# A gated feed-forward kernel whose gated values are stored with three of nine blocks as sums of three, and a last stage in another order

## The chip, the cores and the metric

One core of one Trainium2 chip. The metric is the device time of one execution in microseconds (us); lower is better.

## What is computed

Causal attention with a window of 128 and a linear position bias over 8 batches, 8 heads, 576 positions and 64 dimensions a head; its output, 4608 tokens of 512 features, goes through a gated feed-forward layer of 1536 hidden units. All of it is float32.

```python
gate = 1.0 / (1.0 + np.exp(-(x @ w_gate)))
val = x @ w_val
return (gate * val @ w_out).astype(np.float32)
```

## The kernel before, in words

The order of all work is written by a planner at build time: `Graph` (L97) takes every operation with an engine, an estimated cost, its reads, writes, a rank and a release time, plays them through against engines that each do one thing at a time, and emits the instructions in the order of their planned start. On the chip each engine's queue runs in that order and waits where it must. All plain transfers are issued on SyncE's queue (`move`, L225), the accumulating ones, which add to what lies at their destination, on GpSimd's (L936).

The work has three stages. In the first (to about 294 us) attention is computed in transposed form, and the first four of twelve hidden blocks of 128 (`ffn`, L657) are projected for the first 3072 tokens. GpSimd makes the attention's masks there (L601). In the second (`ffn2`, L797) the rest of the projections runs in five groups of two halves of tokens (three groups of 2 x 512, two of 2 x 384). It works with fast 2 x 2 block products (7 instead of 8, L850), one chunk for each hidden block and group. A chunk takes 42 matmuls. For each half the gate is a tanh on ScalarE (`gate`, L860), the gated value `(tanh + 1) * val` is made on VectorE (`gated`, L864), and `put` (L644) stores it to DRAM, to a scratch array called `hid`. The gated halves lie in buffers `later_hs`: two in turn, four in the last group. The first thing that a later chunk writes there is a copy by ScalarE of a product out of PSUM (L872, with `copy` of L221).

The third stage is `last` (L921), called for three passes `t` of 1536 tokens. It computes the product with `w_out`: six blocks of `w_out` (2 halves of the outputs m by 3 thirds of the hidden units k) against nine blocks of gated values (3 thirds k by 3 blocks of 512 tokens n). This goes by a scheme of 15 block products instead of 18. Each product takes a sum of blocks of `w_out` (made beforehand by `prepare_o`, L736, stored, and fetched by `fetch_o`, L781), and a sum of blocks of gated values, and is accumulated into one of six running sums ("chains" A to F) in PSUM; outputs are combined from these.

A product (L988) consists of 24 matmuls of 128x512 in float32r: two output blocks j, two quarters q, two rows of 128, three high/low combinations. For each quarter ScalarE makes the high part of the input (L996) and VectorE subtracts it for the low part (L997, through the helper `minus`, L230), in a ring of four buffers `duo`, thus two products. `load` (L925) brings a block of gated values (two transfers of 512 KB) to a free slot; eleven slots exist. `more` (L934) adds a second block to it by an accumulating transfer. `sums` (L939) adds or subtracts whole rows on VectorE (two instructions, L942). After a product, `snap` (L962) copies a running sum out on ScalarE, and `plus` (L968) and `both` (L974) combine results on VectorE; `store` (L982) writes an output block.

In the kernel before, five of the fifteen inputs are made by a plain load, an accumulating load on top of it and a subtraction:

```python
load("f", 0, 0)
more("f", 2, 1)
sums("f", "20", "f", sub)
product(5, "A", "f", lambda j: (plus("y00", "A", "b1", j), store("y00", 0, 0, j)))
```

Of the kernel before, what the change touches and what calls it, by code (L numbers as in the profile page):

```python
# [8 lines left out]
F32 = mybir.dt.float32  # L9
# [6 lines left out]
P = 128  # L16
# [26 lines left out]
OUT0, OSTEP = 425.0, 48.0  # L43
# [35 lines left out]
ORDER = (11, 6, 13, 7, 12, 8, 5, 14, 10, 2, 1, 0, 3, 9, 4)  # L79
# [5 lines left out]
           ((4, (1, 1), SUB, (0, 1)), (9, (1, 0), ADD, (1, 1))))  # L85
SINGLES = ((10, (1, 0)), (2, (0, 1)), (5, (0, 2)), (14, (1, 2)))
# [113 lines left out]
def attention_gated_ffn(ctx: ExitStack, tc: tile.TileContext, qd, kd, vd, wg, wv, wo, out):  # L200
# [85 lines left out]
    for p in range(1, NPAIR):  # L286
# [5 lines left out]
    hid = {(k, q, t): dram.tile([P, 2, NB], F32, name=f"hid{k}{q}{t}")  # L292
           for k in range(3) for q in range(2) for t in range(NB9)}
# [349 lines left out]

    def put(fc, a, b, src, keys, F):  # L644
# [12 lines left out]
    def ffn(t, w):  # L657
# [29 lines left out]
        for i0 in range(0, n, GRP):  # L687
            grp = range(i0, min(n, i0 + GRP))
            for i in grp:
                s = project("g", i)  # L690
                sg = lambda i=i: T(moe, f"sg{i % GRP}", [P, NB], F32)
                g.add("ACT", act_cost(wd, psum=True), lambda s=s, sg=sg: nc.scalar.activation(sg()[:, 0:wd], mm[s][:, 0:wd], AF.Tanh, scale=0.5),
                      [("mm", s)], [("sg", i % GRP)], F)
            for i in grp:
                s = project("v", i)
                sg = lambda i=i: T(moe, f"sg{i % GRP}", [P, NB], F32)
                e = slim[0] % 2
                slim[0] += 1
                h = lambda e=e: hs(e, "early_hs")
                g.add("DVE", dve_cost(wd, psum=True), lambda s=s, sg=sg, h=h: nc.vector.scalar_tensor_tensor(  # L700
                    h()[:, 0:wd], sg()[:, 0:wd], 1.0, mm[s][:, 0:wd], op0=ALU.add, op1=ALU.mult), [("sg", i % GRP), ("mm", s)], [("hs", e, 0), ("hs", e, 1)], F)
                put(w.fcs[i], t * NB, end, lambda a, b, h=h: h()[:, a - t * NB:b - t * NB], [("hs", e, 0), ("hs", e, 1)], F)
# [33 lines left out]
    def prepare_o(kt, want, release):  # L736
# [4 lines left out]
        decode(wo, kt, gt, kg, want, release)  # L741
        for k in (1, 2):
            decode(wo, 4 * k + kt, lambda k=k: tt()[:, 2 * k - 2:2 * k].rearrange("p a f -> p (a f)").bitcast(I32), kt0, want, release + step / 3 * k)
# [3 lines left out]
        for n, batch in enumerate(BATCHES):  # L747
# [7 lines left out]
            for o, (p, a, op, b) in enumerate(batch):  # L755
                va, vb, vo = val(a), val(b), val(p)
                g.add("DVE", dve_cost(2 * P, two=True), lambda va=va, vb=vb, vo=vo, op=op: nc.vector.tensor_tensor(vo(), va(), vb(), op=op),
                      [key(a), key(b)], [("wtmp", z, o)], want, port=True, release=release + (n + 1) * step)
            for o, (p, *_) in enumerate(batch):
                y, i = at_o(p, kt)  # L760
                if y < len(SLOTS):
                    move(lambda y=y, i=i: stash_o[y][:, i], lambda v=val(p): v(), [("wtmp", z, o)], [("stash_o", y, i)], want, 128)
                    continue
                hi, lo, v = (lambda o=o, z=z: six(z)[:, o, 0]), (lambda o=o, z=z: six(z)[:, o, 1]), val(p)
                g.add("ACT", act_cost(2 * P), lambda hi=hi, v=v: nc.scalar.copy(hi(), v()), [("wtmp", z, o)], [("wtmp", z, "hi", o)], want)
                g.add("DVE", dve_cost(2 * P, two=True), lambda hi=hi, lo=lo, v=v: nc.vector.tensor_tensor(lo(), v(), as32(hi()), op=SUB),
                      [("wtmp", z, "hi", o)], [("wtmp", z, o)], want, port=True)
                move(lambda y=y, i=i: stash_o[y][:, i:i + 2], lambda z=z, o=o: as32(six(z))[:, o], [("wtmp", z, o), ("wtmp", z, "hi", o)],
                     [("stash_o", y, i)], want, 256)
        for p, y in SINGLES:  # L770
            z, i = at_o(p, kt)
            move(lambda z=z, i=i: stash_o[z][:, i], block[y], [kt0 if y[1] else kg], [("stash_o", z, i)], want, 128)
# [24 lines left out]
    def ffn2(t, w, todo, F, ends=False):  # L797
# [40 lines left out]
        def chunk(i, fc):  # L838
# [21 lines left out]
            def gate(b, h):  # L860
                g.add("ACT", act_cost(N2, psum=True), lambda: nc.scalar.activation(sg[h](), bk(b)(), AF.Tanh, scale=0.5),  # L861
                      [("mm", b)], [("sg", h)], F)
# [58 lines left out]
    def last(t):  # L921
# [3 lines left out]
        def load(name, k, n):  # L925
            slots = [stage_free.pop(0) for _ in range(2)]
            rows[name] = slots
            for q, slot in enumerate(slots):
                move(lambda slot=slot: staged(slot), lambda q=q: hid[k, q, 3 * t + n], hid_keys(k, n, q), [("row", *slot)], F, 512, True)

        def hid_keys(k, n, q):
            return [y for y in g.writer if y[0] == "hid" and y[1] // 2 == 2 * k + q and y[2] == 3 * t + n]

        def more(name, k, n):  # L934
            for q, slot in enumerate(rows[name]):
                g.add("POOL", 1.2, lambda slot=slot, q=q: nc.gpsimd.dma_start(staged(slot), hid[k, q, 3 * t + n], accum_op=ALU.add),  # L936
                      hid_keys(k, n, q), [("row", *slot)], F, size=512 / 300.0, port=False)
# [30 lines left out]
        def plus(o, chain, a, j, scale=0.5):  # L968
            b, va = bks[chain, j], val((a, j))
            g.add("DVE", dve_cost(NB, psum=True), lambda: nc.vector.scalar_tensor_tensor(va(), mm[b], scale, va(), op0=ALU.mult, op1=ALU.add),  # L970
                  [("mm", b)], [key((a, j))], F)
            held_at[o, j] = held_at.pop((a, j))

        def both(o, a, b, op, j):  # L974
            va, vb = val((a, j)), val((b, j))
            g.add("DVE", dve_cost(NB, two=True), lambda: nc.vector.tensor_tensor(va(), va(), vb(), op=op), [key((b, j))], [key((a, j))], F, port=True)
            held_at[o, j] = held_at.pop((a, j))
# [4 lines left out]
        def store(name, m, n, j):  # L982
            r, c = (2 * m + j) * P, (3 * t + n) * NB
# [4 lines left out]
        def product(p, chain, name, then):  # L988
            ring = []
            for q in range(2):  # L990
# [5 lines left out]
                copy(hi, v, 2 * NB, [("row", *slot)], [("ar", r, 0)], F)  # L996
                minus(lo, v, lambda hi=hi: as32(hi()), 2 * NB, [("row", *slot), ("ar", r, 0)], [("ar", r, 1)], F, pool=False)  # L997
# [19 lines left out]
        add, sub = ALU.add, ALU.subtract  # L1017
        load("10", 1, 0)
        product(11, "A", "10", lambda j: snap("a1", "A", j))
        load("00", 0, 0)  # L1020
        product(6, "B", "00", lambda j: snap("b1", "B", j))
        load("21", 2, 1)
        sums("10", "21", "10", sub)
        product(13, "A", "10", lambda j: snap("a2", "A", j))
        drop("10")
        load("22", 2, 2)
        sums("00", "22", "00", sub)
        product(7, "B", "00", lambda j: snap("b2", "B", j))
        drop("00")
        product(12, "A", "21", lambda j: snap("a3", "A", j))  # L1030
        drop("21")
        product(8, "B", "22", lambda j: snap("b3", "B", j))
        drop("22")
        load("20", 2, 0)
        load("f", 0, 0)
        more("f", 2, 1)
        sums("f", "20", "f", sub)
        product(5, "A", "f", lambda j: (plus("y00", "A", "b1", j), store("y00", 0, 0, j)))
        drop("f")
        load("g", 1, 0)  # L1040
        more("g", 2, 2)
        sums("g", "20", "g", sub)
        drop("20")
        product(14, "B", "g", lambda j: (plus("y10", "B", "a1", j), store("y10", 1, 0, j)))
        drop("g")
        load("02", 0, 2)
        load("i", 0, 0)
        more("i", 1, 2)
        sums("i", "02", "i", sub)
        product(10, "C", "i", lambda j: plus("y12", "C", "b3", j))  # L1050
        drop("i")
        load("j", 0, 1)
        more("j", 1, 0)
        load("11", 1, 1)
        sums("j", "11", "j", sub)
        drop("11")
        product(2, "F", "j", lambda j: snap("d1", "F", j))
        drop("j")
        for z in range(len(SLOTS), len(SLOTS) + len(LATER)) if t == 0 else ():
            fetch_o(z)  # L1060
        load("01", 0, 1)
        load("22", 2, 2)
        sums("02", "01", "02", add)
        sums("02", "02", "22", sub)
        drop("22")
        product(1, "C", "02", lambda j: plus("y02", "C", "b2", j))
        drop("02")

        def zero(j):
            plus("dd", "D", "d1", j)  # L1070
            both("y01", "a3", "dd", add, j)
            store("y01", 0, 1, j)
            both("y02", "y02", "dd", sub, j)
            free("dd", j)
        product(0, "D", "01", zero)
        load("12", 1, 2)
        sums("01", "01", "12", add)
        product(3, "F", "01", lambda j: (plus("y02", "F", "y02", j), store("y02", 0, 2, j)))
        drop("01")
        product(9, "E", "12", lambda j: (plus("y12", "E", "y12", j), store("y12", 1, 2, j), plus("a2", "E", "a2", j, -0.5)))  # L1080
        load("k", 1, 1)
        more("k", 1, 2)
        load("21", 2, 1)
        sums("k", "k", "21", sub)
        drop("12", "21")
# [168 lines left out]
```

## Time and profile before

| | |
|---|---|
| Median of 3 runs | 977.18 us (976.1 to 977.45) |
| The profiled execution | 976.8 us |
| Its span, first to last instruction | 975.1 us |
| TensorE, VectorE, ScalarE, GpSimd busy | 950.1, 794.8, 526.6, 162.5 us |
| Last stage, first to last matmul | 698.5 to 970.7 us |
| Moved by DMA | 222.22 MB |

The profile is of one execution. A chain of waits follows back from the last instruction what released each step. Windows give busy time by stretch, with counts of instructions (x), the granted TensorE clock (1.00 is the full 2.4 GHz) and the mean busy share of the 16 DMA engines. A matmul's recorded time overlaps its neighbours', so a busy TensorE need not be at its full rate: the count in a stretch tells that. "Landing" is the time from issue to the end of a transfer.

### The profile page before, as it was taken

To read this page: it belongs to the slowest core of one execution; us is meant where nothing else is said; L and a number is where in the kernel's file an instruction comes from. 1 tells how busy PE (TensorE), PEld (TensorE's weight loads), DVE (VectorE), ACT (ScalarE), POOL (GpSimd) and SP (SyncE) were. 2 spreads that over 40 slices of the span, in tenths; PEclk is the share of its full clock that TensorE was granted. 3 is DMA by queue.
4 is the path that set the end of the run, shared out by engine and by line. 5 is a ranking of instruction groups with operands and counts; after the bars stand their busy time and mean duration, and the time that the engine had idled before them with its cause. 6 is when DMAs were issued, how large, how long until landed. Compare 5 with 4: busy or idle time off the path is not lost.

```text
span 975.1 us, 18738 instructions
## 1 busy us (share of the span) xinstructions
PE 950.1 (97%) x6468; PEld 808.7 (83%) x6468; DVE 794.8 (82%) x1947; ACT 526.6 (54%) x1348; POOL 162.5 (17%) x337
## 2 busy tenths in 40 slices
PE   9999999999999999999999999999997999999898
PEld 7778888888889999999888888888885787778676
DVE  8999788888899899878875877845866996897697
ACT  8988778888865453443533634544531443244231
POOL 3544444444340000000000000000011001001100
PEclk9999999999999999999999999999998899999999
DMA  8787769857654344246555576374799979997992
GB/s 316 271 288 245 240 223 314 297 192 255 220 185 156 115 151 144 79 157 224 195 216 178 174 269 215 130 259 157 268 340 302 294 262 265 334 299 221 264 315 87
DMA packets 96095, 222.22 MB, mean 228 GB/s; under 512 B 10496, under 2 KB 38272, under 8 KB 95616
## 3 DMA queue, kind: packets, MB, share of 16 engines
q1 hardware_dynamic: 91536, 205.16, 60.7%
q0 software_dynamic: 4320, 15.73, 8.4%
q8 instruction: 51, 0.84, 0.3%
q14 instruction: 44, 0.36, 0.1%
q10 hardware_dynamic: 144, 0.13, 0.0%
HBM read 158.86 MB, written 62.13 MB: 227 GB/s over the span
## 4 chain that ended last, share of the span: by engine, by line
PE 75%; DMA 11%; DVE 9%; issue 3%; ACT 1%; POOL 0%; DVEq 0%; POOLq 0%; ACTq 0%
PE mm L850 40%; PE mm L681 14%; DMA rows_xr<-hid 6%; PE mm L1011 6%; PE mm L476 5%; DVE duo L230 4%; PE mm L547 4%; PE mm L590 3%; DMA rows_ar<-hid 3%; DMA rows_hs<-hid 2%; PE mm L628 2%; DVE rows_xr L942 1%; PE mm L307 1%; DVE part_h L970 1%; DVE rows_hs L942 1%
## 5 line engine op out<-in xcount | busy, mean ns | idle before, releaser
L850 PE MATMUL mm<-xc,w2s 128*128 128x384 f32 (+1 forms) x2016 | 404.4, 362 | 0.0
L850 PEld LDWEIGHTS mm<-xc,w2s 128*128 128x128 f32 x2016 | 363.7, 188 | 40.3 <-DVE later_hs L857 0.9
L1011 PE MATMUL mm<-duo,wo 128*128 128x512 f32 x756 | 180.7, 398 | 18.1 <-DVE duo L230 18.1
L1011 PEld LDWEIGHTS mm<-duo,wo 128*128 128x128 f32 x756 | 143.6, 191 | 54.3 <-DVE duo L230 24.2
L681 PE MATMUL mm<-first,first 128*128 128x512 f32 x576 | 156.2, 407 | 0.1
L681 PEld LDWEIGHTS mm<-first,first 128*128 128x128 f32 x576 | 101.2, 188 | 21.3 <-issue 1.1
L861 ACT ACTIVATE sg<-mm 128x384 f32<-128x384 f32 (+1 forms) x96 | 52.4, 547 | 106.3 <-PE mm L850 60.3
L857 DVE TENSOR_TENSOR mm<-mm,low 128x384 f32<-128x384 f32 (+1 forms) x96 | 60.2, 629 | 51.7 <-PE mm L850 50.9
L221 ACT COPY low<-mm 128x512 f32<-128x512 f32 (+1 forms) x93 | 49.8, 538 | 71.0 <-PE mm L850 64.6
L505 ACT ACTIVATE pb<-pb,st 128x128 f32<-128x128 f32 x216 | 85.0, 400 | 2.0 <-DVE st L501 1.7
L936 POOL DMA_DIRECT2D rows_ar<-hid x7 | 6.3, 897 | 375.2 <-DMA rows_ar<-hid 375.2
L601 POOL TENSOR_SCALAR_AFFINE_SELECT pt<-early_h 128x384 f32<-128x384 f32 x96 | 51.1, 551 | 56.3 <-ACT early_h L221 55.9
L601 POOL TENSOR_SCALAR_AFFINE_SELECT pt<-spread 128x384 f32<-128x384 f32 x96 | 53.0, 575 | 42.6 <-ACT spread L221 41.9
L493 DVE COPY_PREDICATED mm<-early_h,mm 128x256 f32<-128x256 int32 (+1 forms) x144 | 48.9, 390 | 3.7 <-PE mm L476 3.7
L547 PEld LDWEIGHTS mm<-pt,vr 64*64 64x64 f32 x1056 | 43.2, 133 | 10.0 <-issue 4.7
L221 ACT CAST duo<-rows_xr 128x1024 fp32r<-128x1024 f32 x29 | 30.4, 1053 | 36.0 <-DVE rows_xr L942 25.8
L501 DVE CUSTOM_DVE_ANT_0 pb<-mm,early_h 128x128 f32<-128x128 f32 x216 | 49.7, 284 | 0.0
L547 PE MATMUL mm<-pt,vr 64*64 64x192 f32 (+2 forms) x1056 | 47.3, 284 | 0.0
L583 DVE TENSOR_SCALAR pb<-pb,st 128x128 f32<-128x128 f32 x169 | 42.3, 297 | 1.3
L230 DVE TENSOR_TENSOR duo<-rows_xr,duo 128x1024 fp32r<-128x1024 f32 x35 | 42.5, 1222 | 0.8 <-ACT duo L221 0.5
L505 ACT ACTIVATION_READ_ACCUMULATOR pb<-pb,st 128x1 f32 x216 | 42.2, 195 | 0.0
L865 DVE SCALAR_TENSOR_TENSOR later_hs<-sg,later_hs 128x384 f32<-128x384 f32 (+1 forms) x48 | 29.9, 623 | 11.8 <-ACT sg L861 11.8
(182 smaller groups left out, 1420.5 us busy)
## 6 DMA issues: line engine op xcount, KB each, us to landing
rows_xr<-hid SPq DMA_DIRECT2D x35, 512.0 KB, 6.3
hid<-later_hs SPq DMA_DIRECT2D x48, 256.0 KB, 2.6
rows_wraw<-hid SPq DMA_DIRECT2D x19, 512.0 KB, 6.7
vr<-in_v_dram SPq DMA_DIRECT2D x32, 288.0 KB, 4.8
rows_hs<-hid SPq DMA_DIRECT2D x16, 512.0 KB, 5.4
rows_ar<-hid SPq DMA_DIRECT2D x16, 512.0 KB, 7.7
wraw<-in_moe_w_gate_dram SPq DMA_DIRECT2D x14, 512.0 KB, 5.1
wraw<-in_moe_w_val_dram SPq DMA_DIRECT2D x14, 512.0 KB, 4.1
```

What stands on the lines that cost most here:

```text
L221: g.add("ACT", act_cost(n, psum), lambda: nc.scalar.copy(out(), src()), reads, writes, want, release=release, slack=slack, ways=[("DVE", d ...
L230: g.add("DVE", dve_cost(n, psum, True), lambda: nc.vector.tensor_tensor(out(), a(), b(), op=ALU.subtract), reads, writes, want, port=not p ...
L493: g.add("DVE", dve_cost((a1 - a0) * P, psum=True), lambda b=b, a0=a0, a1=a1: nc.vector.copy_predicated(quads(b)[:, a0:a1, 1:3], before[:, ...
L501: g.add("DVE", 0.21, lambda: nc.vector.tensor_tensor_reduce(pb()[:, e], sp[b][:, a, D:D + P], relm[u.p][:, w], op0=ALU.add, op1=ALU.min, s ...
L505: g.add("ACT", 0.39, lambda: nc.scalar.activation(pb()[:, e], pb()[:, e], AF.Exp, bias=st()[:, e:e + 1], scale=-1.0, accum_out=st()[:, 3 + ...
L547: nc.tensor.matmul(mm[WORK[h]][e * D:(e + 1) * D, a - e * S - cuts[h]:b - e * S - cuts[h]], vraw(u)[r * D:r * D + D, c], seen, start=first ...
L601: nc.gpsimd.affine_select(pt(u)[:, f0:f0 + 2 * n - 1:2, :], both(), [[0, n], step], cmp, 0.0, base=0, channel_multiplier=mult)
L681: nc.tensor.matmul(mm[s][:, 0:wd], w.tile(kind, wi, i)[:, c * P:(c + 1) * P], xpart(x, c)[:, 0:wd], start=(k == 0 and c == 0), stop=(k == ...
L850: nc.tensor.matmul(mm[b][:, 0:N2], w.tile2(i, wp)[:, wk, c * P:(c + 1) * P], combo(k, xp, N2)[:, c], start=(start and c == 0 and j == 0), ...
L857: g.add("DVE", dve_cost(N2, psum=True), lambda: nc.vector.tensor_tensor(o(), bk(b)(), a(), op=ALU.add), [("mm", b), *reads] if okeys else ...
L861: g.add("ACT", act_cost(N2, psum=True), lambda: nc.scalar.activation(sg[h](), bk(b)(), AF.Tanh, scale=0.5), [("mm", b)], [("sg", h)], F)
L1011: nc.tensor.matmul(mm[b], wo2(z, part_)[:, i, j * P:(j + 1) * P], duo(xp)[:, m], start=start and q == 0 and m == 0 and e == 0, stop=q == 1 ...
```

## The change

The gated values are stored by another set of blocks. `block_of` names the block of a hidden block and a token block by k and n; `LABEL` says which token block takes which n. `HOMES` lists where each is stored: six blocks by themselves, and three sums q2, q5 and q10 of three blocks each. The first block that reaches a sum is stored by a plain transfer, the others are added by accumulating ones (`put`). Three blocks that only enter with a minus (`MINUS`) are made negative when they are gated; where the sign changes within a half, gate and gating are cut in two (`stretches`). The last stage loads the sums as they lie there. Its products come in another order, with other sums of rows and other combinations; running sum D starts as a copy of F (`fork`), and for products 2, 5 and 10 the input is negated as it is split. The accumulating loads are gone. The blocks of `w_out` are indexed to match, all go through five batches, and their release times are a little earlier.

```diff
-OUT0, OSTEP = 425.0, 48.0
+OUT0, OSTEP = 415.0, 46.0
-ORDER = (11, 6, 13, 7, 12, 8, 5, 14, 10, 2, 1, 0, 3, 9, 4)
+ORDER = (11, 2, 13, 0, 12, 3, 5, 4, 9, 6, 10, 7, 1, 8, 14)
...
+LABEL = (1, 2, 0, 0, 1, 2, 2, 1, 0)
+HOMES = {"00": ("00", "q10", "q5"), "01": ("01", "q2"), "02": ("q10",), "10": ("10", "q2"), "11": ("q2",), "12": ("12", "q10"),
+         "20": ("q5",), "21": ("21", "q5"), "22": ("22",)}
+MINUS = ("02", "11", "20")
+
+def block_of(fc, n9):
+    return f"{(fc // 4 + 2) % 3}{LABEL[n9]}"
+
+def sign(fc, n9):
+    return -1.0 if block_of(fc, n9) in MINUS else 1.0
...
     def put(fc, a, b, src, keys, F):
+        kt = fc % 4
         while a < b:
-            t = a // NB
-            e = min((t + 1) * NB, b)
-            move(lambda t=t, a=a, e=e: hid[fc // 4, fc // 2 % 2, t][:, fc % 2, a - t * NB:e - t * NB],
-                 lambda a=a, e=e: src(a, e), keys, [("hid", fc, t, a)], F, (e - a) / 2, True)
+            n9 = a // NB
+            e = min((n9 + 1) * NB, b)
+            t = n9 // 3
+            for h in HOMES[block_of(fc, n9)]:
+                i = a // P
+                while i < e // P:
+                    old, i1 = hid_key(h, t, kt, i % 4) in written, i
+                    while i1 < e // P and (hid_key(h, t, kt, i1 % 4) in written) == old:
+                        i1 += 1
+                    parts_ = [hid_key(h, t, kt, x % 4) for x in range(i, i1)]
...
+                    if old:
+                        g.add("POOL", 1.2, lambda to=to, of=of: nc.gpsimd.dma_start(to(), of(), accum_op=ALU.add), keys, parts_, F,
+                              size=2 * kb / 300.0, port=False)
+                    else:
+                        move(to, of, keys, parts_, F, kb, True)
+                    written.update(parts_)
+                    i = i1
             a = e
...
             def gated(o, val, reads, writes, h, psum):
-                g.add("DVE", dve_cost(N2, psum, True), lambda: nc.vector.scalar_tensor_tensor(
-                    o(), sg[h](), 1.0, val(), op0=ALU.add, op1=ALU.mult), [("sg", h), *reads], writes, F, port=not psum)
+                for x, y, s in stretches(fc, t0 + h * N2, t0 + (h + 1) * N2):
+                    g.add("DVE", dve_cost(y - x, psum, True), lambda x=x, y=y, s=s: nc.vector.scalar_tensor_tensor(
+                        o()[:, x:y], sg[h]()[:, x:y], s, val()[:, x:y], op0=ALU.add, op1=ALU.mult), [("sg", h), *reads], writes, F, port=not psum)
...
+        def fork(chain, new, j):
+            b = bks[chain, j]
+            b2 = bks[new, j] = bank()
+            g.add("ACT", act_cost(NB, psum=True), lambda: nc.scalar.copy(mm[b2], mm[b]), [("mm", b)], [("mm", b2)], F)
...
+                if minus_:
+                    g.add("ACT", act_cost(2 * NB), lambda hi=hi, v=v: nc.scalar.mul(hi(), v(), -1.0), [("row", *slot)], [("ar", r, 0)], F)
+                    g.add("DVE", dve_cost(2 * NB, two=True), lambda hi=hi, lo=lo, v=v: nc.vector.scalar_tensor_tensor(
+                        lo(), v(), -1.0, as32(hi()), op0=ALU.mult, op1=SUB), [("row", *slot), ("ar", r, 0)], [("ar", r, 1)], F, port=True)
...
+        load("10")
+        product(11, "A", "10", lambda j: snap("a1", "A", j))
+        load("q2")
+        product(2, "F", "q2", lambda j: fork("F", "D", j), True)
+        load("21")
+        sums("10", "21", "10", SUB)
+        product(13, "A", "10", lambda j: snap("a2", "A", j))
+        load("01")
+        product(0, "D", "01", lambda j: snap("dd", "D", j))
+        product(12, "A", "21", lambda j: (plus("y01", "A", "dd", j, fresh=True), store("y01", 0, 1, j)))
+        drop("21")
+        load("12")
+        sums("01", "01", "12", ADD)
+        product(3, "F", "01", lambda j: plus("y02", "F", "dd", j, op=SUB))
+        load("q5")
+        product(5, "A", "q5", lambda j: snap("y00", "A", j), True)
+        drop("q5")
+        sums("q2", "01", "q2", SUB)
+        sums("q2", "q2", "10", SUB)
+        product(4, "F", "q2", lambda j: plus("y11", "F", "a2", j))
+        drop("q2")
+        product(9, "E", "12", lambda j: (plus("y11", "E", "y11", j, -0.5), store("y11", 1, 1, j), snap("y12", "E", j)))
+        drop("12")
+        load("00")
+        product(6, "B", "00", lambda j: (plus("y00", "B", "y00", j), store("y00", 0, 0, j)))
+        for z in range(len(SLOTS), len(SLOTS) + len(LATER)) if t == 0 else ():
+            fetch_o(z)
+        load("q10")
+        product(10, "C", "q10", lambda j: plus("y12", "C", "y12", j), True)
+        load("22")
+        sums("00", "22", "00", SUB)
+        product(7, "B", "00", lambda j: plus("y02", "B", "y02", j))
+        sums("q10", "01", "q10", SUB)
+        drop("01")
+        sums("q10", "q10", "00", SUB)
+        product(1, "C", "q10", lambda j: (plus("y02", "C", "y02", j), store("y02", 0, 2, j)))
+        drop("q10")
+        product(8, "B", "22", lambda j: (plus("y12", "B", "y12", j), store("y12", 1, 2, j)))
+        drop("22")
+        load("q5")
+        sums("q5", "10", "q5", SUB)
+        sums("q5", "q5", "00", SUB)
+        drop("10", "00")
+        product(14, "B", "q5", lambda j: (plus("y10", "B", "a1", j), store("y10", 1, 0, j)))
+        drop("q5")
```

## Rows read from the trace of the kernel before

**Rows 1.** The page: busy time of each engine over the span.

```profile
PE 950.1 (97%) x6468; PEld 808.7 (83%) x6468; DVE 794.8 (82%) x1947; ACT 526.6 (54%) x1348; POOL 162.5 (17%) x337
```

**Rows 2.** The chain that ended last, 600 to 975 us: start, length, what.

```profile
599.84 88.89 PE mm L850 x393
...
708.44 13.42 DMA rows_xr<-hid
...
723.49 13.73 DMA rows_xr<-hid
...
833.50 10.82 DMA rows_hs<-hid
...
970.78 0.69 DVE part_h L970
```

**Rows 3.** Stretches of 10 us in the last stage (x: instructions).

```profile
700.00:710.00 10.00, 10.00 (x46) 8.29 (x45) 9.76 (x11) 5.65 (x8) 0.00 (x0) 1.00 1.04 433
740.00:750.00 10.00, 9.73 (x36) 7.50 (x34) 6.75 (x8) 2.10 (x2) 0.88 (x1) 0.83 1.05 273
750.00:760.00 10.00, 5.27 (x12) 3.84 (x12) 6.96 (x7) 2.09 (x2) 0.00 (x0) 0.69 0.97 365
870.00:880.00 10.00, 10.00 (x46) 8.29 (x45) 10.00 (x12) 3.48 (x4) 0.00 (x0) 1.00 1.00 338
```

**Rows 4.** TensorE's timeline, first and last matmuls of the last stage: start, length.

```profile
698.53 38.85 PE L1011 MATMUL mm<-duo,wo 128*128 128x512 f32 x170
...
959.70 11.04 PE L1011 MATMUL mm<-duo,wo_ar 128*128 128x512 f32 x48
```

**Rows 5.** Waits, 688 to 975 us: us in total, times, longest.

```profile
PE mm L1011 <- DVE duo L230: 18.1, 12, 5.0
```

**Rows 6.** DMA queues, 688 to 975 us: packets, MB, share of 16 engines.

```profile
q1 hardware_dynamic: 19144, 62.23, 59.3%
q0 software_dynamic: 4320, 15.73, 28.6%
```

**Rows 7.** Line 936, the accumulating loads: ns min/median/max of an issue; their landing.

```profile
L936 POOL DMA_DIRECT2D rows_wraw<-hid x5: 865/865/1191, 729.8 to 942.2; - x5
...
DMA to landing us min/median/max: 5.4/9.3/13.7
```

**Rows 8.** Instruction groups, 688 to 975 us: count, busy, mean ns, idle before.

```profile
L230 DVE TENSOR_TENSOR duo<-rows_xr,duo 128x1024 fp32r<-128x1024 f32 x35 | 42.5, 1222 | 0.8 <-ACT duo L221 0.5
...
L970 DVE SCALAR_TENSOR_TENSOR part_h<-mm,part_h 128x512 f32<-128x512 f32 x30 | 20.3, 691 | 3.8 <-PE mm L1011 3.8
...
L942 DVE TENSOR_TENSOR rows_xr<-rows_xr 128x1024 f32<-128x1024 f32 x7 | 8.5, 1221 | 2.5 <-DMA rows_xr<-hid 2.5
```

**Rows 9.** Longer stretches: PE, PEld, DVE, ACT, POOL, clock, DMA share.

```profile
100.00:200.00 100.00, 99.91 (x1246) 84.42 (x1242) 82.39 (x405) 79.59 (x309) 41.69 (x99) 1.00 0.80 268
450.00:500.00 50.00, 50.00 (x249) 44.71 (x248) 39.29 (x63) 23.37 (x42) 0.00 (x0) 1.00 0.61 209
550.00:600.00 50.00, 50.00 (x222) 41.37 (x221) 35.97 (x61) 20.70 (x36) 0.00 (x0) 1.00 0.67 232
688.00:975.00 287.00, 264.44 (x1127) 212.45 (x1125) 234.79 (x247) 100.31 (x118) 26.62 (x30) 0.98 0.88 272
```

**Rows 10.** The buffers of gated halves: landing of their stores, whole kernel.

```profile
DMA to landing us min/median/max: 1.6/2.1/16.4
```

**Rows 11.** Timeline of VectorE and ScalarE: gated halves made, and buffers written again.

```profile
435.72 0.56 DVE L865 SCALAR_TENSOR_TENSOR later_hs<-sg,later_hs 128x384 f32<-128x384 f32 x1
...
442.80 0.48 ACT L221 COPY later_hs<-mm 128x384 f32<-128x384 f32 x1 [0.49 <-PE mm L850]
...
613.49 0.69 DVE L865 SCALAR_TENSOR_TENSOR later_hs<-sg,later_hs 128x512 f32<-128x512 f32 x1 [0.63 <-ACT sg L861]
...
625.04 0.59 ACT L221 COPY later_hs<-mm 128x512 f32<-128x512 f32 x1 [0.63 <-PE mm L850]
```

More of the change, by code (lines that the diff above doesn't have):

```diff
@@ L291, in attention_gated_ffn @@
     stash_o += [dram.tile([P, n, 2 * P], F32, name=f"parts_o{z}") for z, (_, _, n) in enumerate(LATER)]
-    hid = {(k, q, t): dram.tile([P, 2, NB], F32, name=f"hid{k}{q}{t}")
-           for k in range(3) for q in range(2) for t in range(NB9)}
+    hid = {(h, t, q): dram.tile([P, 2, NB], F32, name=f"hid{h}{t}{q}")
+           for h in sorted({h for hs_ in HOMES.values() for h in hs_}) for t in range(NB9 // 3) for q in range(2)}
     plain_w = {(kind, i): dram.tile([P, DM], F32, name=f"plain{kind}{i}") for kind in "gv" for i in range(STORED, FC1)}
@@ L641, in attention_gated_ffn, with hid_key, stretches @@
     first_xr = keep("xr", KC, NB)
+    written = set()
+    def hid_key(h, t, kt, i):
+        return "hid", h, t, kt, i
     def put(fc, a, b, src, keys, F):
+        kt = fc % 4
         while a < b:
-            t = a // NB
-            e = min((t + 1) * NB, b)
-            move(lambda t=t, a=a, e=e: hid[fc // 4, fc // 2 % 2, t][:, fc % 2, a - t * NB:e - t * NB],
-                 lambda a=a, e=e: src(a, e), keys, [("hid", fc, t, a)], F, (e - a) / 2, True)
-            a = e
+            n9 = a // NB
[8 more added lines that the diff above has]
+                    parts_ = [hid_key(h, t, kt, x % 4) for x in range(i, i1)]
+                    to = lambda h=h, t=t, i=i, i1=i1: hid[h, t, kt // 2][:, kt % 2, i * P % NB:i * P % NB + (i1 - i) * P]
+                    of = lambda i=i, i1=i1: src(i * P, i1 * P)
+                    kb = (i1 - i) * P / 2
+                    if old:
[5 more added lines that the diff above has]
+                    i = i1
+            a = e
+    def stretches(fc, a, b):
+        got = []
+        for x in range(a, b, P):
+            y = sign(fc, x // NB)
+            if got and got[-1][2] == y:
+                got[-1][1] = x + P
+            else:
+                got.append([x, x + P, y])
+        return [(x - a, e - a, y) for x, e, y in got]
     def hs(e, name="later_hs"):
@@ L923, in last, with load @@
         rows, left = {}, {}
-        def load(name, k, n):
+        def load(name, of=None):
             slots = [stage_free.pop(0) for _ in range(2)]
@@ L928, in load @@
             for q, slot in enumerate(slots):
[L929 to L937, printed above, removed]
+                move(lambda slot=slot: staged(slot), lambda q=q: hid[of or name, t, q],
+                     [hid_key(of or name, t, 2 * q + m, i) for m in range(2) for i in range(4)], [("row", *slot)], F, 512, True)
         def sums(o, a, b, op):
@@ L966, in snap, with plus @@
             g.add("ACT", act_cost(NB, psum=True), lambda: nc.scalar.mul(o(), mm[b], 0.5), [("mm", b)], [key((name, j))], F)
-        def plus(o, chain, a, j, scale=0.5):
-            b, va = bks[chain, j], val((a, j))
[L970 to L977, printed above, removed]
+        def fork(chain, new, j):
+            b = bks[chain, j]
+            b2 = bks[new, j] = bank()
+            g.add("ACT", act_cost(NB, psum=True), lambda: nc.scalar.copy(mm[b2], mm[b]), [("mm", b)], [("mm", b2)], F)
+        def plus(o, chain, a, j, scale=0.5, op=ADD, fresh=False):
+            b, va = bks[chain, j], val((a, j))
+            if fresh:
+                keep_at((o, j))
+                writes, reads = [key((o, j))], [key((a, j))]
+                vo = val((o, j))
+            else:
+                writes, reads, vo = [key((a, j))], [], va
+                held_at[o, j] = held_at.pop((a, j))
+            g.add("DVE", dve_cost(NB, psum=True), lambda: nc.vector.scalar_tensor_tensor(vo(), mm[b], scale, va(), op0=ALU.mult, op1=op),
+                  [("mm", b), *reads], writes, F)
         def free(name, j):
@@ L986, in store, with product @@
             free(name, j)
-        def product(p, chain, name, then):
+        def product(p, chain, name, then, minus_=False):
             ring = []
@@ L1026, in last @@
[L1026 to L1030, printed above, removed]
-        drop("21")
[L1032 to L1054, printed above, removed]
@@ L1060, in last @@
             fetch_o(z)
[L1061 to L1064, printed above, removed]
-        drop("22")
[L1066 to L1085, printed above, removed]
-        product(4, "F", "k", lambda j: (plus("y11", "F", "a2", j), store("y11", 1, 1, j)))
```

54 lines of the change are left out of this document (22 added, 32 removed).

## The prediction

> **What bounds the kernel now.** The first view is the page's busy time: TensorE 97%, VectorE 82% [rows 1]. That is an average, so the next view is the chain of waits in order of time [rows 2]. Up to 688 us its long pieces are matmuls: the attention and the gated projections leave TensorE no gap, and nothing moved there can make them shorter. From 708 us on the chain is mostly loads of 8 to 14 us: the plain one of 708 us released GpSimd's issue of the accumulating one into the same slot, which is the piece of 723 us. So the last stage is where time can be won.
>
> How much? The stretches of 10 us show 46 matmuls in each of 700 to 710 and 870 to 880, but 36 in 740 to 750 and 12 in 750 to 760 [rows 3]. There the granted clock also fell to 0.83 and 0.69 (a mean of the 1.2 and 2.4 GHz levels), right after TensorE had stood idle. The count has to be read, not the busy time, which is 9.73 us with only 36 matmuls. The undisturbed rate comes from the last 48 matmuls [rows 4]: about (11.04 - 0.39)/47 = 0.2266 us each, where 0.39 us is the length of the last one. The stage has 3 passes x 15 products x 24 = 1080 matmuls, 244.7 us at that rate. It ran from 698.53 us to 959.70 + 11.04 = 970.74 us [rows 4], 272.2 us. **27.5 us are lost**; the other 698.5 us before it and 975.1 - 970.7 = 4.4 us behind it (one sum, one store) stay. The waits name the loss: 18.1 us of TensorE's idle time ended with the subtraction that makes the low part of a product's input [rows 5]. The rest is the slow clock (about 4 us: 48 matmuls in 740 to 760 that take some 15 us awake instead of 10.9) and small gaps.
>
> Why are these inputs late? The queues of 688 to 975 us [rows 6]: plain transfers fill 59.3% of 287 us (170 us for 62.23 MB, 366 GB/s), the accumulating ones 28.6% (82 us for 15.73 MB, only 192 GB/s). Together 252 of 287 us. An accumulating load takes 5.4 to 13.7 us to land, 9.3 in the middle [rows 7], and stands behind a plain load of the same slot.
>
> **The change, part by part.**
>
> *Loads of the last stage.* A pass loads 16 sums or blocks of 1 MB plus 5 accumulating ones; after the change it loads 10, all plain. That is 36 plain issues of 512 KB and all 30 accumulating ones fewer. Plain traffic falls by 36 x 0.524 = 18.9 MB to 43.4 MB, 119 us at 366 GB/s, with nothing beside it: under half of a stage of some 250 us. No product then stands behind two transfers in a row. What the loads cost goes from 27.5 us to near nothing; late next is VectorE.
>
> *VectorE in the last stage.* By the code a pass has 30 subtractions for the parts, 20 sums of rows and 22 combinations of results; after, 30, 18 and 20 (the last all read PSUM). At 1.222, 1.22 and 0.69 us [rows 8] that is 36.7 + 24.4 + 15.2 = 76.3 us before, 36.7 + 22.0 + 13.8 = 72.5 us after, so 11.5 us less in three passes: 234.8 us of busy time [rows 9] become about 223, under the 244.7 us of TensorE. In the whole it fits; locally it doesn't quite. The inputs' ring holds two products, so the parts of a product are made while the one before it runs (24 x 0.2266 = 5.4 us). Over products 6, 10, 7, 1 and 8 (27.2 us) I count 10 subtractions (12.2), 7 sums of rows (8.5: two for the input of 7, four for that of 1, one of the four for 14) and 12 combinations (8.3), 29.0 us. That is some 2 us a pass, **6 us** in all. Bounds: 0 (its sums run ahead) and 20 us (VectorE's waits take the place of most of what the loads cost).
>
> *ScalarE.* 7 x 2 copies out of PSUM a pass become 5 x 2 and 2 of the fork, which copies one running sum to a second bank. It was busy 100 of 287 us [rows 9]: nothing. Negated inputs are multiplied by -1 in the instructions that already stand there: nothing. A fork that came late would hold products 0 and 3, but product 13 (5.4 us) stands between it and 0.
>
> *Stores of the gated values.* By the loops of the code there are 145 plain stores (144 before) and 96 new accumulating ones on GpSimd's queue: 8 in the attention, 48 in the groups of 384 columns, 40 in those of 512; 18.9 MB. One issue takes 0.87 us of GpSimd [rows 7], 84 us in all. From 400 us on GpSimd has nothing else (0.00 us busy [rows 9]), so there it delays nobody by its issue. In the attention 8 x 0.87 = 7 us stand among work that fills 42% of it; those waiting for its masks have 58% of slack as cover, and without it each issue would cost up to 0.87 us: 0, at most 7.
>
> Engine time of the transfers: 18.9 MB at 192 GB/s are 98 us. Of this 8.4 MB, 44 us, fall into the last 150 us before the last stage, where the share was 0.67 [rows 9]; 0.29 more brings it to about 0.96. Plain stores landed in 2.1 us there and earlier [rows 10]; the accumulating ones will be nearer to the 5.4 to 9.3 us of rows 7. What hides them is the time that a gated half may stay in its buffer. In a chunk of 512 columns the half is made by 613.49 + 0.69 and its buffer is written again at 625.04: 10.9 us. In one of 384 it is 435.72 + 0.56 to 442.80: 6.5 us [rows 11]. Issue and landing of 0.87 + 5.4 = 6.3 us fit both, barely the second. Of the 37 chunks with accumulations (5 in group 3, 12 in group 4, 4, 8 and 8 in the groups of 512), those of hidden blocks 8 to 11 in group 4 put three behind each other, the last waiting for the landing of the first on the same bytes. GpSimd's queue behind it holds only further stores; ScalarE's copy into that buffer waits, and the next copies behind it keep a bank from TensorE. I take **3 us** for this; bounds: 0 (it all fits) and 15 us (0.4 us in each of the 37).
>
> *The rest.* 16 gatings of 384 columns are cut in two where the sign changes: 16 more instructions each on ScalarE and VectorE, at some 0.15 us of fixed cost each (0.56 and 0.69 us for 384 and 512 columns [rows 11]), under engines with room. The output weights are prepared 10 to 16 us earlier, the same number of them; the matmuls' count is the same. Nothing.
>
> **The sum**: 698.5 + 244.7 + 4.4 = 947.6 us of span without any loss; + 6 + 3 = 956.6; the profiled execution took 1.7 us more than its span (976.8 against 975.1): **958 us**, 19 less. It is 0.4 us under the median of the runs, 977.18, and I add nothing for that.
>
> **Rivals.**
>
> *VectorE takes over.* Its sums and parts are late wherever loads were. For it: it is already the last link of every wait of TensorE [rows 5]. Against it: in 870 to 880 us it was busy all 10.00 us and TensorE still made its 46 matmuls [rows 3]. With the upper bound of 20 us: 947.6 + 20 + 3 + 1.7 = 972. Chance 0.12.
>
> *The stores push back a little.* Accumulations cost 10 to 15 us in the projections: 965 to 970, still faster. Chance 0.09.
>
> *Slower: the gated buffers are held too long.* Place: ScalarE's copy into a reused half, in the 37 chunks with accumulations. Price: the median landing, 9.3 us, plus two issues of 0.87 is 11.0 us; over the room that is 4.5 us in each of 17 chunks of 384 and 0.1 us in 20 of 512: 78 us, of which some 2 us a chunk may be taken up by the banks in hand; 2.5 x 17 = 43 us, so 958 - 3 + 43 = 998. It decides from a hold of about 9.8 us in the 384s (3.3 - 2 = 1.3 us x 17 = 22 us). Against it: the 9.3 us is for 512 KB on engines that were full, these are 64 to 256 KB on engines at 0.61 [rows 9]. The Trainium skill ("SBUF — State Buffer", section "SBUF: two separate sides") says that GpSimd cannot write a DMA's descriptors while VectorE runs a two-port copy, 3.1 us instead of 0.62; as an estimate from that page each such meeting would add 2.5 us to a hold, 0.3 us beyond room and banks in a 384, and the sum would be 963 with one in each of the 17. The trace does not show it: beside a VectorE busy 82% of the time, 30 such issues took 0.865 us and at most 1.19 [rows 7, 9]. Chance 0.08.
>
> *It does not do what it says.* The inputs are late for VectorE's own order, not the loads, and nothing comes of it: 977. The pieces of 13 us in the chain [rows 2] speak against it. Chance 0.03.
>
> **How the numbers follow.** The forecast has 0.68, with its own range of 949 to 966. About 0.2%, 2 us, is what a measurement of this kernel can tell from no change. Faster by more: 0.68 + 0.12 + 0.09 = 0.89; within: 0.03; slower: 0.08. The range goes from 949, where both unknown costs vanish, to 972, which takes in the first two rivals; it leaves out the last two.
>
> **What would show it.** In the changed profile: no accumulating load, the hardware queue's share of the last stage near a half, 46 matmuls in nearly every 10 us with the clock at 1.00, 96 accumulating stores on GpSimd, last product of the projections still ending near 698 to 702 us. Wrong it would be if ScalarE's copy waits for stores of gated values add up to more than a few us with gaps of TensorE behind them, or if TensorE's waits for the subtraction stay near 18 us with no load in the chain.

## The result, and the profile after

The changed kernel takes **965.07 us** in the median of 4 runs (962.45 to 966.88), the kernel before 976.84 us in the same comparison: a ratio of 0.9878, interval 0.9849 to 0.9907. It is faster by 11.8 us, where 19 were forecast; 958 was predicted with a range of 949 to 972. The profiled execution took 966.62 us, its span 964.9 us.

TensorE's timeline of the changed kernel (start, length, what, count, and the idle time before with its releaser) shows where the time came from and where it went.

```profile
295.78 11.72 PE L894 MATMUL mm<-xc,w2s 128*128 128x384 f32 x66
...
371.46 12.76 PE L894 MATMUL mm<-xc,w2s 128*128 128x384 f32 x72 [1.73 <-ACT later_hs L233]
...
584.67 51.80 PE L894 MATMUL mm<-xc,w2s 128*128 128x512 f32 x215 [1.83 <-DMA w2s<-stash]
...
669.27 20.71 PE L894 MATMUL mm<-xc,w2s 128*128 128x512 f32 x90 [0.95 <-DVE later_hs L234]
...
717.57 54.56 PE L1061 MATMUL mm<-duo,wo 128*128 128x512 f32 x240
...
950.13 11.04 PE L1061 MATMUL mm<-duo,wo_ar 128*128 128x512 f32 x48
```

Line 894 makes the projections' matmuls (850 before), line 1061 the last stage's (1011 before). The projections start at 295.78 us instead of 294.39 (so the chain of waits has it; the timeline has 294.32), and the last stage's unbroken run of 1074 matmuls starts at 717.57 and ends at 961.17 us. Six of its matmuls run ahead among the projections, so the projections took 717.57 - 295.78 - 6 x 0.2266 = 420.4 us instead of 404.1. The account of the span is:

| Part | before | after | |
|---|---|---|---|
| attention | 294.4 | 295.8 | +1.4 |
| projections | 404.1 | 420.4 | +16.3 |
| last stage, 1080 matmuls | 272.2 | 245.0 | -27.2 |
| behind the last matmul | 4.4 | 3.7 | -0.7 |

Stretches as in rows 3, ahead of them three of the projections, in the changed kernel (after the times PE, PEld, DVE, ACT, POOL with counts, then clock, DMA share, GB/s):

```profile
330.00:340.00 10.00, 10.00 (x60) 10.00 (x59) 8.84 (x16) 3.15 (x7) 0.74 (x1) 1.00 0.52 160
...
370.00:380.00 10.00, 8.54 (x49) 8.55 (x50) 8.50 (x17) 3.78 (x10) 1.74 (x2) 1.00 0.61 131
...
580.00:590.00 10.00, 7.29 (x21) 5.25 (x20) 1.37 (x2) 1.18 (x2) 2.05 (x3) 0.69 1.07 325
...
740.00:750.00 10.00, 10.00 (x46) 8.27 (x45) 7.67 (x9) 3.18 (x3) 0.00 (x0) 1.00 0.50 156
750.00:760.00 10.00, 10.00 (x46) 8.28 (x45) 7.22 (x9) 1.50 (x3) 0.00 (x0) 1.00 0.64 213
...
870.00:880.00 10.00, 10.00 (x46) 8.29 (x45) 9.40 (x11) 4.67 (x5) 0.00 (x0) 1.00 0.97 366
```

The last stage now has its 46 matmuls in each of these stretches. The gaps and the clock's fall to 0.69 are found in the projections: in 580 to 590 us only 21 matmuls ran, after an idle wait for a weight fetch. Of the shorter matmuls of 384 columns 60 fit into 330 to 340 us, and 49 into 370 to 380. The chain that ended last (start, length, what) answers to rows 2. It now has its long transfers ahead of the last stage, from the weight fetch of 570 us on:

```profile
570.64 13.98 DMA w2s<-stash
...
617.89 9.02 DMA hidq<-later_hs
...
653.98 14.47 DMA parts_o<-wtmp
...
717.73 243.45 PE mm L1061 x1074
...
961.21 0.69 DVE part_h L1021
```

The waits of 290 to 720 us (who waited <- for whom: us in total, times, longest) name two kinds above all:

```profile
ACT later_hs L233 <- DMA hidq<-later_hs: 22.8, 14, 2.8
...
PE mm L894 <- ACT later_hs L233: 3.6, 4, 1.7
PE mm L894 <- DMA w2s<-stash: 2.7, 2, 1.8
PE mm L894 <- ACT low L233: 2.3, 6, 0.8
```

ScalarE's copy into a buffer of gated halves waits for the halves' stores to land, which in the kernel before it did for 4.1 us in the same stage. The other wait is for the fetched weights. The chain shows a third place: the store of 653.98 us, of prepared output weights, held one of the two tiles that the last group takes as further buffers of gated halves. The copy into it came late, and TensorE stood idle before 669.27 us. The queues of 296 to 720 us (packets, MB, share of 16 engines) and the 88 accumulating stores of the projections (line 678: ns min/median/max of an issue, then their landing):

```profile
q1 hardware_dynamic: 41913, 73.72, 51.7%
q0 software_dynamic: 12384, 16.26, 27.3%
```

```profile
L678 POOL DMA_DIRECT2D hidq<-later_hs x88: 847/865/2151, 361.8 to 720.2; - x88
...
DMA to landing us min/median/max: 2.7/5.5/12.2
```

27.3% of 424 us is 116 us for 16.26 MB: **140 GB/s**. In the view of stretches the DMA share of the projections went from 0.53 (294.4 to 698.5 us) to 0.79 (296 to 720 us).

### The profile page after: what moved, and what is told of

It is laid out like the page before. It is cut to its first block, busy times and chain, and to the rows that moved or that the text cites. A ratio compares the mean times of both kernels' runs of the same rounds, so it can differ in the third digit from the quotient of the medians.

```text
span 964.9 us, 18826 instructions
## 1 busy us (share of the span) xinstructions
PE 949.3 (98%) x6468; PEld 808.9 (84%) x6468; DVE 789.9 (82%) x1958; ACT 517.1 (54%) x1352; POOL 220.9 (23%) x402
## 3 DMA queue, kind: packets, MB, share of 16 engines
q0 software_dynamic: 13824, 18.88, 13.7%
## 5 line engine op out<-in xcount | busy, mean ns | idle before, releaser
L894 PE MATMUL mm<-xc,w2s 128*128 128x384 f32 (+1 forms) x2016 | 411.2, 364 | 9.6 <-ACT later_hs L233 3.6
L1061 PE MATMUL mm<-duo,wo 128*128 128x512 f32 x756 | 172.5, 389 | 0.0
L678 POOL DMA_DIRECT2D hidq<-later_hs x88 | 78.2, 968 | 290.7 <-DVE later_hs L911 187.0
L906 ACT ACTIVATE sg<-mm 128x512 f32<-128x512 f32 (+3 forms) x112 | 53.5, 492 | 99.1 <-PE mm L894 55.7
L233 ACT COPY low<-mm 128x384 f32<-128x384 f32 (+1 forms) x94 | 50.1, 534 | 79.2 <-PE mm L894 64.0
L613 POOL TENSOR_SCALAR_AFFINE_SELECT pt<-early_h 128x384 f32<-128x384 f32 x96 | 53.5, 578 | 58.9 <-ACT early_h L233 56.4
L901 DVE TENSOR_TENSOR later_hs<-mm,later_hs 128x384 f32<-128x384 f32 (+1 forms) x48 | 29.8, 621 | 25.6 <-ACT later_hs L233 16.9
L233 ACT COPY later_hs<-mm 128x384 f32<-128x384 f32 (+1 forms) x46 | 24.6, 534 | 33.0 <-DMA hidq<-later_hs 22.8
L233 ACT COPY early_h<-mm 128x384 f32<-128x384 f32 (+3 forms) x74 | 31.6, 443 | 17.9 <-PE mm L559 10.3
```

What stands on the lines that cost most here:

```text
L233: g.add("ACT", act_cost(n, psum), lambda: nc.scalar.copy(out(), src()), reads, writes, want, release=release, slack=slack, ways=[("DVE", d ...
L613: nc.gpsimd.affine_select(pt(u)[:, f0:f0 + 2 * n - 1:2, :], both(), [[0, n], step], cmp, 0.0, base=0, channel_multiplier=mult)
L678: g.add("POOL", 1.2, lambda to=to, of=of: nc.gpsimd.dma_start(to(), of(), accum_op=ALU.add), keys, parts_, F, size=2 * kb / 300.0, port=False)
L894: nc.tensor.matmul(mm[b][:, 0:N2], w.tile2(i, wp)[:, wk, c * P:(c + 1) * P], combo(k, xp, N2)[:, c], start=(start and c == 0 and j == 0), ...
L901: g.add("DVE", dve_cost(N2, psum=True), lambda: nc.vector.tensor_tensor(o(), bk(b)(), a(), op=ALU.add), [("mm", b), *reads] if okeys else ...
L906: g.add("ACT", act_cost(y - x, psum=True), lambda x=x, y=y, s=s: nc.scalar.activation(sg[h]()[:, x:y], bk(b)()[:, x:y], AF.Tanh, scale=0.5 ...
```

## Experiments

Two theories of the 16.3 us: HOLD (a gated half's buffer is not free when it is wanted) and ENGINES (the added transfers fill the DMA engines, and others come late). A rival, PLAN, has neither: another order of the work costs it. The numbers below are medians; ratios are to the kernel before in the same comparison.

**1. The accumulating stores left out.**

```diff
                     if old:
-                        g.add("POOL", 1.2, lambda to=to, of=of: nc.gpsimd.dma_start(to(), of(), accum_op=ALU.add), keys, parts_, F,
-                              size=2 * kb / 300.0, port=False)
+                        pass
```

> The changed kernel with the 96 accumulating stores left out (each sum then holds only its first block, so the output is not the layer's). The projections took 16.3 us more than before the change and the attention 1.4 us. Theory HOLD (a gated half cannot be written again until its last, slower store has landed) and theory ENGINES (the added transfers fill the DMA engines and make other transfers late) both say that all of this goes: 947 to 950 us. Rival PLAN (the planner's new order of the work, the other release times of the output weights, or the cut gatings cost it): 960 us or more.

Measured: 951.6 us, 0.9743 (0.9728 to 0.9757). That is 1.6 us above what both theories gave and far below PLAN's 960: 13.5 us hang on these 96 stores (965.07 - 951.6; the profiled execution of the changed kernel was 1.5 us above its median, so its 16.3 us are at the upper end).

**2. The same stores as plain transfers.**

```diff
-                        g.add("POOL", 1.2, lambda to=to, of=of: nc.gpsimd.dma_start(to(), of(), accum_op=ALU.add), keys, parts_, F,
+                        g.add("POOL", 1.2, lambda to=to, of=of: nc.gpsimd.dma_start(to(), of()), keys, parts_, F,
```

> The 96 stores stay on GpSimd's queue, at their places and with their waits, but are plain transfers that overwrite instead of adding (so the sums are not formed). ENGINES: an accumulating byte took nearly twice the engine time of a plain one (192 against 366 GB/s), so about half of the added engine time goes and with it over half of the loss: 954 to 958 us. HOLD: issue, queue and landing stay nearly as they are: 961 to 965 us.

Measured: 951.5 us, 0.9744 (0.9729 to 0.9758), the same as without them. The edit changes nothing that the planner sees: by the traces VectorE's 1958 and ScalarE's 1352 instructions come in the same order as in the changed kernel, so PLAN falls here. Neither 96 more transfers, nor 18.9 MB more, nor their issue on GpSimd cost anything that can be told; **that they add** costs it all. This run's queue in its own projections, 296 to 704 us, and line 678 in it:

```profile
q0 software_dynamic: 5344, 16.26, 10.6%
```

```profile
L678 POOL DMA_DIRECT2D hidq<-later_hs x88: 537/539/1180, 361.7 to 706.1; - x88
...
DMA to landing us min/median/max: 1.9/3.6/9.6
```

The same bytes took 10.6% of 408 us = 43 us of the engines, 376 GB/s against 140, in 5344 packets against 12384. They landed in 3.6 instead of 5.5 us, and an issue took 0.54 instead of 0.87 us. The time lies below what either theory gave. Both are still open, since faster transfers help both; the expectation of HOLD, that issue and landing stay as they are, was wrong.

**3. A third buffer for the half that is written first.**

```diff
+    mixed = lambda: T(moe, "mixed", [P, 4 * NB], F32R, tag="h4")
...
-            a1, u2, p5, v5 = lambda: low()[:, 2], lambda: low()[:, 3], lambda: hs(e)[:, 1, 0:N2], lambda: hs(e)[:, 0, 0:N2]
+            e3 = e if ends else turns[0] % 3
+            second = lambda: as32(mixed())[:, 12 * P:] if e3 == 2 and not ends else hs(e3)[:, 1]
+            a1, u2, p5, v5 = lambda: low()[:, 2], lambda: low()[:, 3], lambda: second()[:, 0:N2], lambda: hs(e)[:, 0, 0:N2]
```

(The buffer is the unused end of a tile in which the output weights are prepared.)

> A third buffer for the second half of a chunk, the one that a later chunk writes first: it gets one more chunk (7 us at 384 columns, 9.5 at 512) to land its stores. Nothing else is changed. HOLD: the 8 us lost in the groups of 384 columns go almost wholly and ScalarE's waits for stores of gated halves (22.8 us) fall under 5: 956 to 959 us. ENGINES: 963 to 966 us.

Measured: 957.85 us, 0.9817 (0.9788 to 0.9847), just clear of the changed kernel's interval. The waits of its projections:

```profile
ACT later_hs L233 <- DMA hidq<-later_hs: 5.3, 3, 2.9
```

22.8 us became 5.3, and the time fell by 7.2 us, about half of the loss, as HOLD said. The planner also wrote another order here (it moved eight copies from ScalarE to VectorE), and what that alone does isn't shown.

**4. The chunk of the fetched weights run last in two groups.**

```diff
-        ffn2(t, w2, head[1:] + [(0, here)] + body, FIRST + 1, ends)
+        ffn2(t, w2, head[1:] + ([(0, here)] + body if ends else body + [(0, here)]), FIRST + 1, ends)
```

> In the first two groups of 512 columns the chunk whose weights are fetched back runs last instead of third of the rest, so that the fetch has four more chunks (38 us) to land. ENGINES: the stop of TensorE at 580 to 590 us, where that fetch took 14 us to land, goes, with its slow clock: about 5 us, 959 to 961 us. HOLD: that stop is not the stores' doing through a buffer, but it would go as well; if the projections are held by buffers alone the time stays at 964 to 966 us.

Measured: 962.28 us, 0.9858 (0.9842 to 0.9875). It is 2.8 us less, between the two expected ranges; the intervals overlap, and waits for such fetches of 1.7 us were left. So this is the direction of ENGINES and not proof of it.

**5. Both.**

> The third buffer for the second half and the chunk of the fetched weights run last, together. If the two losses lie in different places (buffers held in the groups of 384 columns, late transfers in those of 512), they add: 7 us and 3 us off 965, 954 to 956 us, and this would beat both kernels. If both act on the same waits: 957 to 958 us.

Measured: 955.32 us, 0.9789 (0.9763 to 0.9815): 9.8 us less than the changed kernel, the sum of the two (7.2 + 2.8 = 10.0).

**6. Both, and the output weights prepared earlier.**

```diff
-OUT0, OSTEP = 415.0, 46.0
+OUT0, OSTEP = 395.0, 44.0
```

> The same, and the output weights are released for preparation earlier (at 395 us, 44 us apart, instead of 415 and 46), so that their loads and stores leave the stretch of 550 to 650 us, where the DMA engines are full. ENGINES: 1 to 3 us less than third_fetch, 952 to 954 us. If they only collide with the accumulating stores of the groups of 384 columns instead: the same or up to 3 us more.

Measured: **951.97 us**, 0.9747 (0.9724 to 0.9771), the fastest of the versions that compute the whole layer: 25 us less than before the change and 13 less than the changed kernel. Its projections, TensorE's timeline and the queues of 296 to 700 us:

```profile
295.56 402.59 PE L897 MATMUL mm<-xc,w2s 128*128 128x384 f32 x2010
```

```profile
q1 hardware_dynamic: 41660, 72.02, 52.9%
q0 software_dynamic: 12329, 16.18, 27.4%
```

2010 matmuls without a gap. The accumulating stores still take 27.4% of 404 us = 111 us of the engines. So their engine time can be hidden; it is being waited for that costs. How much of the last 3.4 us is the earlier release isn't settled: the intervals of 5 and 6 overlap.

The traces of these runs (one execution each) show where the time went. The projections are split at their first matmul of 512 columns; the six matmuls of the last stage among them are taken off:

| us | before | changed | plain stores (2) | third buffer (3) | fetch last (4) | both (5) | both, weights earlier (6) |
|---|---|---|---|---|---|---|---|
| to the first of 512 columns | 174.3 | 182.0 | 175.4 | 175.3 | 179.4 | 174.4 | 174.2 |
| from there on | 229.9 | 238.5 | 230.4 | 236.1 | 234.6 | 232.8 | 229.6 |

The third buffer wins mainly in the groups of 384 columns, the later fetch in those of 512. But fetch last is also 2.6 us shorter in the first row, where its order of work is still that of the changed kernel: so much can be the spread of executions.

**7. The release times of before.**

> The changed kernel with the release times of the output weights put back to what they were before the change (425 us, 48 apart). Rival PLAN gave these a part in the loss. If they do nothing: 963 to 967 us. If the earlier release helped: 967 to 970 us. If it hurt: under 962 us.

Measured: 962.92 us, 0.986 (0.983 to 0.9891), within the changed kernel's interval. The release times in the change did neither harm nor good that can be told. In its profiled execution (965.96 us) ScalarE waited 8.9 us for the stores of gated halves, against 22.8: the sum of these waits is not by itself the time lost.

**8. The eight stores in the attention left out.**

> Only the 8 accumulating stores of the attention stretch are left out (the sum q5 then lacks these blocks). The attention ended 1.4 us later than before the change. If GpSimd's 8 issues of 0.88 us delay the masks: the projections start at 294.4 us instead of 295.8, and 963 to 964 us. If the 1.4 us comes from the planner's other order: 295.5 to 296 us and 964 to 966 us.

Measured: 962.78 us, 0.9858 (0.983 to 0.9887), which can't be told from the changed kernel. The projections start at 296.65 us, outside both expected ranges, but this execution was late from its beginning. TensorE's timeline in this run:

```profile
19.53 2.13 PE L640 MATMUL mm<-pt,vr 128*64 128x256 f32 x28
...
296.65 73.67 PE L896 MATMUL mm<-xc,w2s 128*128 128x384 f32 x420
```

The same first matmuls of line 640 in the changed kernel:

```profile
17.19 2.13 PE L640 MATMUL mm<-pt,vr 128*64 128x256 f32 x28
```

From these matmuls to the projections it takes 277.1 us here and 278.6 in the changed kernel. Over all twelve profiles it is 277.0 to 277.2 us in the five without these stores (the kernel before and experiments 1, 8, 9 and 10) and 278.2 to 279.3 in the seven with them, plain ones too. So the attention's 1.4 us hang on the eight stores. Whether their issues cost them or the order that the planner writes around them (VectorE's differs from 150 us on) isn't separated.

**9 and 10. The kernel before without its accumulating loads, and with them as plain ones.** Here the gain is put to the test: which loads did the 27.5 us hang on?

```diff
-            for q, slot in enumerate(rows[name]):
+            for q, slot in ():
```

> The kernel before the change with its 30 accumulating loads of the last stage left out (five inputs of each pass are then incomplete); the 96 plain loads, the sums and the combinations stay. It lost 27.5 us there. If the accumulating loads carried the loss (their engine time of 82 us, and two loads one behind the other): under 8 us stay, 950 to 957 us. If the number of plain loads alone does it (62 MB at 366 GB/s are 170 us of some 250): 958 to 968 us. If VectorE's own order does it: over 968 us.

Measured: 948.94 us, 0.9724 (0.9709 to 0.9738). With all 96 plain loads and all of VectorE's work in place, nothing is lost, 245.0 us from the first matmul of the last stage to the last:

```profile
698.31 55.92 PE L1011 MATMUL mm<-duo,wo 128*128 128x512 f32 x246
...
932.23 11.04 PE L1011 MATMUL mm<-duo,wo_ar 128*128 128x512 f32 x48
```

> The kernel before the change with the same 30 loads as plain transfers that overwrite instead of adding, with the same queue and waits. If the cost of an accumulating load is that it comes second into its slot: 972 to 977 us, as before the change. If it is the engine time (192 against 366 GB/s, 39 us less of it): half of the loss or more goes, 955 to 965 us.

Measured: 957.84 us, 0.9822 (0.9801 to 0.9842), with VectorE's and ScalarE's work in the order of the kernel before. Its queue in 688 to 956 us, and TensorE's wait there (18.1 us before [rows 5]):

```profile
q0 software_dynamic: 4320, 15.73, 15.9%
```

```profile
PE mm L1011 <- DVE duo L230: 4.2, 4, 2.7
```

15.9% of 268 us is 43 us, 369 GB/s instead of 192. Of the 27 us that before_none wins, plain transfers in the same places win 18; the other 9 are what 30 more loads, second into their slots, cost at the plain price.

## Why the prediction was right or wrong

*The place and the sign* were right: all of the gain is in the last stage, and TensorE's floor of 244.7 us for it was reached (245.0).

*The loads of the last stage.* That their cost would go to near nothing held. The reason was half right: the prediction set 36 plain loads and 30 accumulating ones against the engines together. Experiments 9 and 10 show that the plain ones were harmless by themselves: without the accumulating loads nothing is lost, and two thirds of the loss came from adding. One reading of the loss was off: beside the waits of 18.1 us and some 4 us of slow clock it had "small gaps", but those waits are all of TensorE's idle time in that stage; the 5 us left lie in the matmuls themselves.

*VectorE in the last stage, 6 us*: too much. 0.3 us was lost. Its busy time there was 218.7 us of 715 to 961 us, near the 223 worked out. The local surplus of some 2 us a pass came from a wrong reading: instructions were priced by their lengths. The stretch of products 6, 10, 7, 1 and 8 in the second pass, and some of VectorE's instructions in it:

```profile
846.80:874.00 27.20, 27.20 (x122) 22.52 (x121) 26.67 (x29) 11.06 (x12) 0.00 (x0) 1.00 0.72 228
```

```profile
855.89 1.21 DVE L981 TENSOR_TENSOR rows_xr<-rows_wraw,rows_xr 128x1024 f32<-128x1024 f32 x1
857.02 1.22 DVE L981 TENSOR_TENSOR rows_hs<-rows_hs,rows_xr 128x1024 f32<-128x1024 f32 x1
858.15 0.68 DVE L1021 SCALAR_TENSOR_TENSOR part_sg<-mm,part_sg 128x512 f32<-128x512 f32 x1
858.75 1.21 DVE L981 TENSOR_TENSOR rows_xr<-rows_xr,rows_tt 128x1024 f32<-128x1024 f32 x1
```

The 29 instructions are as many as were counted. But they start 1.13 and 0.60 us apart, though they last 1.22 and 0.69: 17 x 1.13 + 12 x 0.60 = 26.4 us, not 29.0, and that fits into 27.2. The kernel before had the same spacing:

```profile
873.17 1.23 DVE L230 TENSOR_TENSOR duo<-rows_xr,duo 128x1024 fp32r<-128x1024 f32 x1
874.30 1.23 DVE L230 TENSOR_TENSOR duo<-rows_ar,duo 128x1024 fp32r<-128x1024 f32 x1
```

The evidence against that rival, 10.00 us of VectorE beside 46 matmuls [rows 3], was the better guide.

*The stores of the gated values, 3 us, at most 15*: this is the term that failed. They cost 13.5 us by experiment 1, in projections that took 16.3 us more. The prediction's own signs of it came: ScalarE's copies waited 22.8 us with gaps of TensorE behind them, and the projections ended at 717.6 us, not near 698 to 702. Three points of its working were wrong. First, the engine price was taken from accumulating loads into on-chip buffers (192 GB/s); accumulating stores into DRAM went at 140. Second, the smallest landing (5.4 us) was set against the room of 6.5 us; the stores' median was 5.5 us, but with up to three issues of 0.87 us ahead and a tail up to 12.2 us the copies waited 14 times, 22.8 us in all. Third, only the held buffers were priced, and the rest of the transfers at a share near 1 were not: the weight fetch that landed at 584 us, with the slow clock behind it, had no term. The "stores push back a little" rival, at 0.09, is what came to pass: 13.5 us lies within its 10 to 15, the profiled 16.3 a little beyond. That the time came out at the lower end of what it said (965 to 970) is in part luck. The span came out 8.3 us above the sum's 956.6: the projections took 13.3 us more than the 3 allowed and the attention 1.4 more, but VectorE 5.7 less than its 6 and the end 0.7 less.

*The slower rival* named the right place, ScalarE's copy into a reused half. Its price of up to 4.5 us in each of 17 chunks was too high: 22.8 us of waits in all, and TensorE's idle time that ended with a copy of ScalarE was 5.9 us (3.6 + 2.3). Where VectorE's two-port copies lock GpSimd out of writing descriptors, the Trainium skill ("SBUF — State Buffer", section "SBUF: two separate sides") has a transfer take 3.1 us instead of 0.62. This trace does not show that: the 88 issues took 0.865 us in the middle and 2.15 at most, and the runs do not show what made that longest one long.

*Nothing for the rest*: the fork and the negated inputs stand in a last stage without a gap, and with plain stores the projections, cut gatings and all, took 1.6 us more than before. The eight stores in the attention were put at 0, at most 7; they go with 1.4 us (experiment 8).

## What to carry to other kernels

Before a sum is moved into the transfers, compare the same transfers with and without adding: here 18.9 MB of additions on the way to DRAM cost 13.5 us, and the same bytes without adding nothing; with one more buffer and an earlier fetch the additions were hidden too (952.0 us against 951.5). When a transfer gets slower but TensorE has the time, look for what waits for it (a buffer reused two chunks later, a fetch two chunks ahead) and give that one more turn. A stage that looks full of transfers may hang on the few slow ones among them. And before an engine is called too full, price its instructions by the distance of their starts in a busy stretch, not by their lengths.

## What the runs showed of the hardware

An accumulating transfer took far more of the engines than a plain one: into on-chip buffers it went at 192 GB/s and into DRAM at 140, where the same issues without adding went at 369 and 376. GpSimd's issue of a store took 0.87 us instead of 0.54.

By the queue's line in the pages of the profiles, the 96 stores took 13824 packets, 144 each, and 6144 as plain transfers. The 30 loads of the kernel before took 4320, also 144 each, with adding [rows 6] and without (experiment 10). So the number of packets does not explain why the loads are slower with adding; what does is not shown.

VectorE's instructions of 1.22 and 0.69 us, one right behind the other, started 1.13 and 0.60 us apart.
